# First-layer experts in order of their counts, with narrower column blocks, and a buffer fill moved into the recurrence

## The chip, the cores and the metric

The program runs on one core of one Trainium2 chip. The metric is the device time of one execution in microseconds. The kernel before took 592.91 us (median of 3 runs, 591.63 to 594.31).

## The reference

Three stages follow one another. A linear recurrence with state (4 batches, 8 heads, 768 steps, head size 48) gives 3072 tokens of 384 values. A first mixture of experts skips about half of the tokens and sends each of the others to one of 8 experts. A second mixture sends every token to one of 8 experts and keeps only the gated expert output.

```python
state = w[None, :, :, None] * state + np.einsum('bhd,bhe->bhde', kt, vt)   # per step
do_compute = x @ w_skip > 0                    # first mixture only
e_idx = np.argmax(xc @ w_gate, axis=1)
h = np.maximum(xc[mask] @ w1[e], 0.0)          # 384 -> 1024
y[mask] = gate_w[mask, None] * (h @ w2[e])     # 1024 -> 384
out[do_compute] = xc + y                       # second mixture: out[mask] = gate * y
```

With the inputs drawn here, 1490 tokens are not skipped. The first mixture's experts get 190, 182, 205, 159, 189, 184, 188 and 193 of them. Of expert 0's tokens, 126 lie in the first 2048 and 64 behind. The tokens of the second mixture's expert 0 are 188 skipped ones and 175 others.

## The kernel before, in words

The tokens of an expert are gathered through memory. `route` works out a slot for each token, and indirect DMAs from the POOL queue (`scatter`, line 271) write the rows into the buffers `xs1` (first mixture, 256 slots for each expert) and `xs2` (second mixture). The slots that get no token must hold the empty row `zrow`, so both buffers are first filled with it (`prefill`, line 256, on the SP queue). `xs1` is filled in iterations 3 to 8 of the recurrence, in 16 blocks of 128 rows. `xs2` has 29 such blocks; 13 are filled in `first_expert` and 16 in job 1.

The recurrence (`attention`) runs 24 iterations of 128 tokens. Each one loads its r, k and v on the SP queue (lines 439 and 443), several iterations ahead.

The experts run as a list of `jobs`. Expert 0 of the first mixture is done by `first_expert` in plain float32, 160 slots early and 96 late. Jobs 1 to 7 are the other seven experts with 256 slots each, jobs 8 and 9 the two halves of the second mixture's expert 0 (256 slots each), job 10 its expert 1 with 448 slots, and jobs 11 to 16 its experts 2 to 7 in the order of their counts (`by_count`), with 448 to 384 slots.

A job splits each operand into a high and a low float32r part. `gemm1` (line 1059) does 8 groups of 9 products (3 blocks of the contraction, 3 pairs of parts), with a block of 128x128 weights as the stationary operand and the job's slots as the moving columns, so 72 products whose width is the number of slots. `gemm2` (line 1082) does 24 products for each tile of up to 128 slots, with the slots as the stationary operand and 384 moving columns: 48 for two tiles. After each small group `work` is called. It converts one piece of the next expert's weights (`conv_w`, lines 877 and 878), starts the load of the one after (`load_w`, lines 858 and 860), runs steps of `route`, loads the rows of the next job (`load_rows`, line 1022, at step k = 2) and transposes them (`trans`, line 1034, from k = 9 on).

The order on each engine and queue is the order of the program text. The SP queue therefore handles weights, rows and fills strictly in turn, and an entry that waits holds back all behind it. If a count is over its slots, a flag sends the run to the slow path `general`.

Of the kernel before, what the change touches and what calls it, by code (L numbers as in the profile page):

```python
# [24 lines left out]
E = 8  # L25
# [31 lines left out]
PRE2A = 13  # L57
PF2 = range(1, 16, 2)
# [124 lines left out]
def attn_moe_moe_kernel(ctx: ExitStack, tc: tile.TileContext, t, out):  # L183
# [29 lines left out]
    eid = const.tile([1, NR], I32, name="eid")  # L213
    wg = const.tile([128, KB, WGC], F32, name="wg")
# [14 lines left out]
    def setup_consts2():  # L229
        P.iota(rev, pattern=[[-1, 8]], base=8, channel_multiplier=0, allow_small_or_imprecise_dtypes=True)  # L230
        P.memset(ecap, NOSLOT)
        for v in range(3):
            P.iota(ecap[0:1, v, 0:8], pattern=[[CAP1, 8]], base=0, channel_multiplier=0, allow_small_or_imprecise_dtypes=True)
            P.iota(ecap[0:1, v, 8:16], pattern=[[CAP2, 8]], base=2 * CAPS - CAP2, channel_multiplier=0, allow_small_or_imprecise_dtypes=True)
            P.memset(ecap[0:1, v, 8:9], float(CAPS if v == 2 else 0))
        P.memset(ecap[0:1, 1, 0:1], float(CAPA))
        P.memset(cum, 0.0)
        P.memset(caps[:, 1:8], float(CAP1))
        P.memset(caps[:, 9:16], float(CAP2))
        P.memset(caps[:, 0:1], float(CAPL))  # L240
        P.memset(caps[:, 17:18], float(CAPA))
        P.memset(caps[:, 8:9], float(CAPS))
        P.memset(caps[:, 18:19], float(CAPS))
# [3 lines left out]
        for i, c in enumerate(CAPR):  # L247
            P.memset(caps_r[:, i:i + 1], float(c))
# [155 lines left out]
    def attention():  # L404
        with ExitStack() as actx:
# [321 lines left out]
            for n in range(NT):  # L727
# [105 lines left out]
    def expert(n):  # L833

        if n not in regs:
            r = n - 2 * E + NR
            regs[n] = nc.values_load(eid[0:1, r:r + 1], engines=[mybir.EngineType.SP], min_val=E - NR, max_val=E - 1)
        return regs[n]

    def load_w(n, j):  # L840
# [4 lines left out]
        if n >= 2 * E - NR:  # L845
            e = expert(n)
# [35 lines left out]
    def post1(rows, i, m, p):  # L882
        V.scalar_tensor_tensor(
            out=rows[:, i, 0:DM], in0=p, scalar=rows[:, i, G1:G1 + 1], in1=rows[:, i, 0:DM], op0=ALU.mult, op1=ALU.add)
# [12 lines left out]
    def post2(rows, cap, k, i, m, p):  # L897
        o = rows[0:m, i, 0:DM]
        g = rows[0:m, i, G2:G2 + 1]
        if k == 0:  # L900
            nf, half = divmod(cap, 128)
# [4 lines left out]
        if m < 128:  # L906
# [4 lines left out]
        else:  # L911
            A.activation(out=o, in_=p, func=ACTF.Copy, scale=g)  # L912
# [7 lines left out]
    def first_rows(a, b):  # L920
        for i in range(2):
            lo, hi = max(a, i * 128), min(b, i * 128 + 128)
            if lo < hi:
                nc.sync.dma_start(out=rows0[lo - i * 128:hi - i * 128, i], in_=xs1[lo:hi])
# [18 lines left out]
    def first_2(i, q):  # L943
        if q == 0:
            acc[0] = psf.tile([128, 512], F32, tag="g2", bufs=2, name="g2")[:, 0:DM]
        for fb in (2 * q, 2 * q + 1):
            T.matmul(acc[0], lhsT=h0[:, fb, i * 128:i * 128 + 128], rhs=stage[0, 3 + fb // 3][:, fb % 3], start=fb == 0, stop=fb == FB - 1)
        if q == 3:
            post1(rows0, i, 128, acc[0])
# [3 lines left out]
    def first_expert():  # L953
# [30 lines left out]
        first_T(ps_g.tile([128, 512], F32, tag="tp", name="f_ps"), (0, 1, 2), CAPA, CAP1)  # L984
        for fb in range(FB):
            first_1(fb, CAPA, CAP1)
# [12 lines left out]
    jobs = [(0, n, n * CAP1, CAP1) for n in range(E)] + [(1, E, 0, CAPS), (1, E, CAPS, CAPS)]  # L999
# [5 lines left out]
    def tiles_of(cap):  # L1005

        nf, half = divmod(cap, 128)
# [5 lines left out]
    def load_rows(j):  # L1013
        l, n, base, cap = jobs[j]
        nf, half = divmod(cap, 128)
        small = j <= LAST_S
        x = pools["rows" if small else "rows2"].tile([128, nf + (half > 0), ROW], F32, tag="rows", bufs=3 if small else 2, name="rows")
        eng = nc.sync
        if base is None:
            base = expert(n) * CAP2 + (2 * CAPS - CAP2)  # L1020
# [6 lines left out]
    def trans(j, kb):  # L1027
        l, n, base, cap = jobs[j]
        if kb == 0:
            ps = (first, pools["rows"]) if j <= LAST_S else (pools["rows2"],) * 2  # L1030
            xT[j] = tuple(p.tile([128, KB, cap], F32R, tag=t, bufs=1, name=t) for p, t in zip(ps, ("xh", "xl")))
        tp = ps_g.tile([128, 512], F32, tag="lt" if kb == 1 else "tp", name="xt_ps")
        for i, m in tiles_of(cap):
# [6 lines left out]
    def gemm1(j, fb):  # L1040
# [5 lines left out]
        full = cap - cap % 128  # L1046
        if fb == 0:
# [7 lines left out]
            hT[j] = [p.tile([128, FB, full], F32R, tag=t, bufs=1, name=t) for p, t in zip(ps, ("hh", "hl"))] + extra  # L1055
# [10 lines left out]
    def gemm2(j, k, i, m, q):  # L1066
# [8 lines left out]
        for fb in (2 * q, 2 * q + 1):  # L1075
            if m < 128:
# [4 lines left out]
            for x, (a, b) in enumerate(((hh, w2h), (hh, w2l), (hl, w2h))):  # L1081
                T.matmul(p, lhsT=a[:, fb, r], rhs=b[:, fb], start=(fb == 0 and x == 0), stop=(fb == FB - 1 and x == 2))  # L1082
        if q == 3:
            if l:
                post2(rows[j], cap, k, i, m, p)
# [33 lines left out]
    def work(j, k):  # L1119
# [4 lines left out]
        big = len(tiles_of(cap))  # L1124
# [32 lines left out]
    def job(j):  # L1157
# [4 lines left out]
        for k, (i, m) in enumerate(tiles_of(cap)):  # L1162
# [4 lines left out]
    def by_count(tot):  # L1167

        over = ids_p.tile([1, 19], F32, tag="over", name="over")
        key, rank, place, c = (ids_p.tile([1, 1, NR], F32, tag=n, name=n)[:, 0] for n in ("key", "rank", "place", "cnt"))  # L1170
        m, s = (ids_p.tile([1, NR, NR], F32, tag=n, name=n) for n in ("m", "s"))
        last = slice(2 * E - NR, 2 * E)
# [5 lines left out]
        V.tensor_tensor(out=over, in0=tot, in1=caps, op=ALU.is_gt)  # L1178
        yield "dve"
        V.tensor_copy(out=c, in_=tot[:, last])  # L1180
        yield "dve"
        V.scalar_tensor_tensor(out=key, in0=c, scalar=8.0, in1=key_i, op0=ALU.mult, op1=ALU.add)
# [11 lines left out]
        V.tensor_copy(out=eid, in_=place)  # L1194
        yield "dve"
        V.tensor_tensor(out=s, in0=m, in1=rows_(c), op=ALU.mult)
# [3 lines left out]
        V.tensor_tensor(out=place, in0=place, in1=caps_r, op=ALU.is_gt)  # L1200
        yield "dve"
        V.tensor_tensor(out=over[:, last], in0=over[:, last], in1=place, op=ALU.max)
# [3 lines left out]
    with tc.manual_schedule():  # L1206
# [15 lines left out]
        start(by_count(tot))  # L1222
# [47 lines left out]
```

## Time and profile before

| what | value |
|---|---|
| median of 3 runs | 592.91 us (591.63 to 594.31) |
| the profiled execution: its time, its span | 599.21 us, 597.5 us |
| TensorE busy, mean granted clock | 564.1 us (94%), 0.962 |
| VectorE, ScalarE, GpSimd busy | 361.0, 269.2, 207.1 us |
| recurrence (up to the first product of the first expert) | up to 167.7 us |
| first expert | 167.7 to 194.4 us |
| jobs 1 to 9 | 194.4 to 379.4 us |
| jobs 10 to 16 | 379.4 to 586.5 us |

All times within the run are counted from the start of the span. TensorE's busy share counts a product until its modelled end, so products overlap; the pace of the engine is read from the distance of two starts. The tables of stretches give for each the busy time of every engine, the granted clock of TensorE (1.00 is 2.4 GHz, 0.50 is 1.2 GHz) and the share of the 16 DMA engines in use.

### The profile page before, as it was taken

What the parts mean: (1) busy time and instruction counts of PE and PEld (TensorE: products, weight loads), DVE (VectorE), ACT (ScalarE), POOL (GpSimd) and SP (SyncE); (2) the same over time, 40 slices, a digit from 0 to 9 for tenths busy, and PEclk for the clock granted to TensorE, in tenths of its full rate; (3) what the DMA queues carried; (4) which work ended last, traced back from release to release, by engine and by line L of the source; (5) the groups of instructions that cost most, each with busy time, mean ns of one, the idle gap of its engine ahead of it and who ended that gap; (6) DMA issues with size and microseconds to landing.
All of it is one profiled execution on the core that took longest, in us unless ns stands there. A gap on an engine that the chain in (4) does not pass through costs nothing. (4 is left out here: it accounts for less than half of the span.)

```text
span 597.5 us, 14565 instructions
## 1 busy us (share of the span) xinstructions
PE 564.1 (94%) x5947; PEld 508.0 (85%) x5947; DVE 361.0 (60%) x749; ACT 269.2 (45%) x536; POOL 207.1 (35%) x215
## 2 busy tenths in 40 slices
PE   7999889999989889999999999999999999999992
PEld 4788778788777789999899899998989898999992
DVE  7999999999344638666766635443334345455210
ACT  6344444443244535545564425544534454545320
POOL 6532144351332113688742412223231404142301
PEclk8889999889789989999999999999999999999997
DMA  7858755590535996577766631676466574742100
GB/s 157 206 151 265 227 160 144 165 303 15 181 120 161 356 378 199 203 240 234 240 204 214 199 112 71 195 245 209 154 186 214 150 255 143 255 140 78 38 15 27
DMA packets 57484, 107.66 MB, mean 180 GB/s; under 512 B 7052, under 2 KB 40840, under 8 KB 57408
## 3 DMA queue, kind: packets, MB, share of 16 engines
q1 hardware_dynamic: 51504, 94.82, 51.3%
q0 software_dynamic: 5904, 11.82, 5.3%
q8 instruction: 49, 0.80, 0.6%
q14 instruction: 27, 0.22, 0.1%
HBM read 85.86 MB, written 26.96 MB: 189 GB/s over the span
## 5 line engine op out<-in xcount | busy, mean ns | idle before, releaser
L1059 PE MATMUL g<-xh,w1h 128*128 128x256 f32 (+3 forms) x384 | 122.8, 320 | 0.0
L1059 PE MATMUL g<-xh,w1l 128*128 128x256 f32 (+3 forms) x384 | 120.0, 312 | 0.0
L1059 PE MATMUL g<-xl,w1h 128*128 128x256 f32 (+3 forms) x384 | 119.5, 311 | 0.1
L1061 DVE SCALAR_TENSOR_TENSOR hl<-g,hh 128x256 fp32r<-128x256 f32 (+1 forms) x128 | 61.3, 482 | 89.7 <-ACT hh L1060 87.0
L1082 PE MATMUL g<-w2h,hh 128*128 128x384 f32 x312 | 110.0, 353 | 0.0
L1082 PE MATMUL g<-w2h,hl 128*128 128x384 f32 x312 | 106.1, 340 | 0.0
L1082 PE MATMUL g<-w2l,hh 128*128 128x384 f32 x312 | 105.8, 339 | 0.0
L1060 ACT ACTIVATE hh<-g 128x256 fp32r<-128x256 f32 (+1 forms) x128 | 55.2, 432 | 65.9 <-PE g L1059 61.6
L1059 PEld LDWEIGHTS g<-xh,w1h 128*128 128x128 f32 x384 | 72.1, 188 | 4.5 <-DVE hl L1061 1.6
L878 POOL TENSOR_TENSOR w1l<-s,w1h 128x1024 fp32r<-128x1024 f32 x14 | 33.5, 2394 | 119.8 <-issue 108.7
L1059 PEld LDWEIGHTS g<-xl,w1h 128*128 128x128 f32 x384 | 72.3, 188 | 1.5 <-DVE xl L1038 0.3
L1059 PEld LDWEIGHTS g<-xh,w1l 128*128 128x128 f32 x384 | 72.2, 188 | 1.3
L271 POOL DMA_INDIRECT xs<-xall,idx_all x48 | 54.1, 1128 | 43.0 <-DVE cum L349 30.0
L1082 PEld LDWEIGHTS g<-w2h,hh 128*128 128x128 f32 x312 | 59.8, 192 | 3.1 <-issue 3.0
L1082 PEld LDWEIGHTS g<-w2l,hh 128*128 128x128 f32 x312 | 59.4, 191 | 0.1
L271 POOL DMA_INDIRECT out<-rows,ids x30 | 29.2, 974 | 87.0 <-ACT rows L912 62.3
L1082 PEld LDWEIGHTS g<-w2h,hl 128*128 128x128 f32 x312 | 59.0, 189 | 0.0
L1038 DVE TENSOR_TENSOR xl<-xt_ps,xh 128x256 fp32r<-128x256 f32 (+3 forms) x48 | 23.8, 496 | 55.5 <-ACT xh L1037 55.5
L539 POOL TENSOR_TENSOR RKP<-RK 112x512 f32<-112x512 f32 x22 | 30.4, 1382 | 71.4 <-DMA RK<-in_rk 47.4
L878 DVE TENSOR_TENSOR w1l<-s,w1h 128x1024 fp32r<-128x1024 f32 x28 | 34.3, 1226 | 20.9 <-ACT w1h L877 18.4
L878 DVE TENSOR_TENSOR w2l<-s,w2h 128x1152 fp32r<-128x1152 f32 x28 | 37.9, 1354 | 14.5 <-ACT w2h L877 14.0
L1037 ACT CAST xh<-xt_ps 128x256 fp32r<-128x256 f32 (+3 forms) x48 | 20.8, 433 | 54.7 <-PE xt_ps L1034 51.9
(196 smaller groups left out, 1081.5 us busy)
## 6 DMA issues: line engine op xcount, KB each, us to landing
s<-in_w1b SPq DMA_DIRECT2D x24, 512.0 KB
s<-in_w1a SPq DMA_DIRECT2D x21, 512.0 KB
RK<-in_rk SPq DMA_DIRECT2D x48, 192.0 KB
KV<-in_kv SPq DMA_DIRECT2D x24, 384.0 KB
s<-in_w2b SPq DMA_DIRECT2D x16, 576.0 KB
s<-in_w2a SPq DMA_DIRECT2D x14, 576.0 KB
w2r<-in_w2b SPq DMA_DIRECT2D x5, 1536.0 KB
xs<-zrow SPq DMA_DIRECT2D x7, 582.0 KB
```

Source lines behind the costliest of these rows:

```text
L271: i = P.indirect_dma_start(out=dst, out_offset=bass.IndirectOffsetOnAxis(ap=idx_col, axis=0), in_=src, in_offset=None, bounds_check=last, ...
L539: (V if n < 2 else P).tensor_tensor(out=RKP[x][0:112], in0=RK[i][:, 0], in1=RK[i][:, 1], op=ALU.mult)
L878: (P if j in POOL_LO else V).tensor_tensor(out=lo, in0=x, in1=hi.bitcast(F32), op=ALU.subtract)
L1037: A.copy(out=hi, in_=tp[:, 0:cap])
L1038: V.tensor_tensor(out=lo, in0=tp[:, 0:cap], in1=hi.bitcast(F32), op=ALU.subtract)
L1059: T.matmul(p, lhsT=a[:, kb, f], rhs=b[:, kb], start=(kb == 0 and i == 0), stop=(kb == KB - 1 and i == 2))
L1060: A.activation(out=hh[:, fb], in_=p[:, 0:full], func=ACTF.Relu)
L1061: V.scalar_tensor_tensor(out=hl[:, fb], in0=p[:, 0:full], scalar=0.0, in1=hh[:, fb].bitcast(F32), op0=ALU.max, op1=ALU.subtract)
L1082: T.matmul(p, lhsT=a[:, fb, r], rhs=b[:, fb], start=(fb == 0 and x == 0), stop=(fb == FB - 1 and x == 2))
```

## The change

It has four parts.

1. The number of computed slots in the first mixture becomes 240 for expert 1 and 256, 240, 224, 208, 208, 192 for experts 2 to 7, which are now taken in the order of their counts. The two halves of the second mixture's expert 0 get 240 each. The late part of expert 0 gets 80 in place of 96. The second tile of these jobs has 64 to 128 slots. Places in memory stay as they were.
2. For that order, a ranking of the six counts (`rank_1`) is put in `first_expert`, between the two parts of expert 0: one product and eleven small VectorE operations on one partition. SP reads the ranks into registers (`expert`), as it did for the second mixture.
3. All 29 blocks of `xs2` are filled one by one in iterations 8 to 22 of the recurrence, and no longer in `first_expert` and job 1.
4. The early rows of expert 0 are loaded from the POOL queue and no longer from SP.

```diff
-CAPA, CAPL = 160, 96
-CAPS = 256
+CAPA, CAPL = 160, 80
+CAPS, CAPT = 256, 240
+CAPR1 = (256, 240, 224, 208, 208, 192)
-PRE2A = 13
-PF2 = range(1, 16, 2)
+PF2 = range(8, 23)
...
-                first_rows(0, CAPA)
+                first_rows(0, CAPA, P)
...
                 if n in PF1:
                     q = PF1.index(n)
                     prefill(xs1, PRE1 * q // len(PF1), PRE1 * (q + 1) // len(PF1))
+                if n in PF2:
+                    q = PF2.index(n)
+                    for i in range(PRE2 * q // len(PF2), PRE2 * (q + 1) // len(PF2)):
+                        prefill(xs2, i, i + 1)
...
-            r = n - 2 * E + NR
-            regs[n] = nc.values_load(eid[0:1, r:r + 1], engines=[mybir.EngineType.SP], min_val=E - NR, max_val=E - 1)
+            ei, r = (eid1, n - E + NR) if n < E else (eid, n - 2 * E + NR)
+            regs[n] = nc.values_load(ei[0:1, r:r + 1], engines=[mybir.EngineType.SP], min_val=E - NR, max_val=E - 1)
...
         while not late[0]:
             drain()
             work(())
+        rank_1()
...
-            prefill(xs2, PRE2A * q // 4, PRE2A * (q + 1) // 4)
...
-    jobs = [(0, n, n * CAP1, CAP1) for n in range(E)] + [(1, E, 0, CAPS), (1, E, CAPS, CAPS)]
+    jobs = [(0, n, n * CAP1, CAPT) for n in range(E - NR)] + [(0, E - NR + r, None, c) for r, c in enumerate(CAPR1)]
+    jobs += [(1, E, 0, CAPT), (1, E, CAPS, CAPT)]
...
-            if j == 1 and k in PF2:
-                q, m = PF2.index(k), PRE2 - PRE2A
-                prefill(xs2, PRE2A + m * q // len(PF2), PRE2A + m * (q + 1) // len(PF2))
...
+    def rank_1():
+        tot = ps_g.tile([1, 19], F32, tag="lt", name="tot1")
+        T.matmul(tot, lhsT=ones[:, 0:1], rhs=cum, start=True, stop=True)
+        for _ in by_count(tot[:, E - NR:E], eid1, over1, caps_r1):
+            pass
```

## Rows read from the trace of the kernel before

**Rows 1.** Timeline of TensorE, products: start us, us, engine, line, operation, tiles, count.
```profile
204.31 0.34 PE L1082 MATMUL g<-w2h,hh 128*128 128x384 f32 x1
...
206.24 0.34 PE L1082 MATMUL g<-w2h,hl 128*128 128x384 f32 x1
211.01 0.48 PE L1034 MATMUL xt_ps<-ident,rows 128*128 128x128 f32 x2 [4.43 <-DMA rows<-xs]
...
220.23 0.36 PE L1059 MATMUL g<-xh,w1h 128*128 128x256 f32 x1
...
230.07 0.34 PE L1082 MATMUL g<-w2h,hh 128*128 128x384 f32 x1
...
239.83 0.36 PE L1059 MATMUL g<-xh,w1h 128*128 128x256 f32 x1
```

**Rows 2.** Table of stretches: PE, PEld, DVE, ACT, POOL busy, granted clock, DMA, GB/s.
```profile
195.00:201.50 6.50, 6.50 (x56) 5.90 (x56) 3.64 (x6) 4.53 (x10) 0.00 (x0) 1.00 1.06 345
211.00:214.80 3.80, 3.79 (x14) 3.76 (x14) 1.78 (x2) 1.43 (x2) 0.00 (x0) 0.55 1.05 382
```

**Rows 3.** Timeline of the SP queue, 188 to 201 us.
```profile
188.04 1.29 SPq L858 DMA_DIRECT2D s<-in_w1a  x3
189.38 2.25 SPq L256 DMA_DIRECT2D xs<-zrow  x4
...
199.84 1.04 SPq L256 DMA_DIRECT2D xs<-zrow  x1
200.93 0.46 SPq L1022 DMA_DIRECT2D rows<-xs  x1
```

**Rows 4.** Timeline of TensorE: first and last start of two runs of gemm1.
```profile
199.97 0.28 PE L1059 MATMUL g<-xl,w1h 128*128 128x256 f32 x1
...
201.86 0.28 PE L1059 MATMUL g<-xh,w1l 128*128 128x256 f32 x1
...
379.60 0.36 PE L1059 MATMUL g<-xl,w1h 128*128 128x448 f32 x1
...
387.90 0.37 PE L1059 MATMUL g<-xh,w1h 128*128 128x448 f32 x1
```

**Rows 5.** Timeline of TensorE: plain float32 products of the first expert.
```profile
172.82 2.63 PE L940 MATMUL g<-x,s 128*128 128x160 f32 x18
...
176.47 5.32 PE L947 MATMUL g<-s,h 128*128 128x384 f32 x16
```

**Rows 6.** Timeline of ScalarE: first and last of eight evictions, late part of expert 0.
```profile
183.80 0.25 ACT L941 ACTIVATE h<-g 128x96 f32<-128x96 f32 x1 [1.00 <-PE g L940]
...
188.49 0.25 ACT L941 ACTIVATE h<-g 128x96 f32<-128x96 f32 x1 [0.42 <-PE g L940]
```

**Rows 7.** Table of stretches in the recurrence, columns as in Rows 2.
```profile
58.50:65.00 6.50, 5.63 (x143) 4.78 (x140) 6.35 (x14) 1.77 (x5) 1.36 (x2) 1.00 0.85 263
...
91.00:97.50 6.50, 6.50 (x179) 5.80 (x177) 6.36 (x14) 2.92 (x7) 1.88 (x2) 1.00 0.45 117
```

**Rows 8.** Timelines of SP and ScalarE: last load of v, and its use.
```profile
126.03 0.57 SPq L443 DMA_DIRECT2D KV<-in_kv  x1
...
144.26 0.51 ACT L546 COPY VSO<-KV 64x384 f32<-64x384 f32 x1
```

**Rows 9.** Timelines of POOL, SP and TensorE: early rows of expert 0.
```profile
150.64 0.98 POOL L271 DMA_INDIRECT xs<-xall,idx_all  x1 [0.30 <-issue]
...
153.09 0.80 SPq L924 DMA_DIRECT2D rows<-xs  x2
...
162.74 1.37 PE L934 MATMUL f_ps<-ident,rows 128*128 128x128 f32 x6
```

**Rows 10.** Timeline of VectorE: its idle time in the first expert; one ranking operation.
```profile
190.49 0.43 DVE L1038 TENSOR_TENSOR xl<-xt_ps,xh 128x256 fp32r<-128x256 f32 x1 [4.96 <-ACT xh L1037]
...
364.14 0.18 DVE L1192 TENSOR_REDUCE place<-s 1x6 f32<-1x36 f32 x1
```

**Rows 11.** Instructions of one line: duration min/median/max ns, first and last start us.
```profile
L837 SPq TENSOR_LOAD <-eid x6: 269/278/478, 364.8 to 510.0; - x6
```

More of the change, by code (lines that the diff above doesn't have):

```diff
@@ L883, in post1 @@
         V.scalar_tensor_tensor(
-            out=rows[:, i, 0:DM], in0=p, scalar=rows[:, i, G1:G1 + 1], in1=rows[:, i, 0:DM], op0=ALU.mult, op1=ALU.add)
+            out=rows[0:m, i, 0:DM], in0=p[0:m], scalar=rows[0:m, i, G1:G1 + 1], in1=rows[0:m, i, 0:DM], op0=ALU.mult, op1=ALU.add)
         if i:
@@ L895, in attn_moe_moe_kernel, with post2 @@
     ids = {}
-    def post2(rows, cap, k, i, m, p):
+    def post2(rows, cap, k, i, m, p, small):
         o = rows[0:m, i, 0:DM]
@@ L905, in post2 @@
                 V.tensor_copy(out=ids[0][0:half, nf], in_=rows[0:half, nf, IDC:IDC + 1])
-        if m < 128:
+        if m < 128 and not small:
             A.copy(out=o, in_=p[m:2 * m])
@@ L1003, in attn_moe_moe_kernel, with row_tiles, tiles_of @@
     rows, xT, hT, pools, done = {}, {}, {}, {}, set()
-    def tiles_of(cap):
+    def row_tiles(cap, small):
+        return (2, 0) if small else divmod(cap, 128)
+    def tiles_of(j):
+        cap = jobs[j][3]
+        if j <= LAST_S:
+            return [(0, 128), (1, cap - 128)]
         nf, half = divmod(cap, 128)
@@ L1045, in gemm1 @@
         f = slice(fb * 128, fb * 128 + 128)
-        full = cap - cap % 128
+        full = cap if j <= LAST_S else cap - cap % 128
         if fb == 0:
@@ L1075, in gemm2 @@
         for fb in (2 * q, 2 * q + 1):
-            if m < 128:
+            if m < 128 and j > LAST_S:
                 ng = 128 // m
@@ L1081, in gemm2 @@
             for x, (a, b) in enumerate(((hh, w2h), (hh, w2l), (hl, w2h))):
-                T.matmul(p, lhsT=a[:, fb, r], rhs=b[:, fb], start=(fb == 0 and x == 0), stop=(fb == FB - 1 and x == 2))
+                T.matmul(p[0:m], lhsT=a[:, fb, r], rhs=b[:, fb], start=(fb == 0 and x == 0), stop=(fb == FB - 1 and x == 2))
         if q == 3:
             if l:
-                post2(rows[j], cap, k, i, m, p)
+                post2(rows[j], cap, k, i, m, p, j <= LAST_S)
             else:
@@ L1165, in job, with by_count @@
                 work(j, FB + 4 * k + q)
-    def by_count(tot):
-        over = ids_p.tile([1, 19], F32, tag="over", name="over")
-        key, rank, place, c = (ids_p.tile([1, 1, NR], F32, tag=n, name=n)[:, 0] for n in ("key", "rank", "place", "cnt"))
+    def by_count(c, ei, few, slots):
+        key, rank, place, cnt = (ids_p.tile([1, 1, NR], F32, tag=n, name=n)[:, 0] for n in ("key", "rank", "place", "cnt"))
         m, s = (ids_p.tile([1, NR, NR], F32, tag=n, name=n) for n in ("m", "s"))
-        last = slice(2 * E - NR, 2 * E)
         def rows_(x):
@@ L1177, in by_count @@
         yield "dve"
-        V.tensor_tensor(out=over, in0=tot, in1=caps, op=ALU.is_gt)
+        V.tensor_copy(out=cnt, in_=c)
         yield "dve"
-        V.tensor_copy(out=c, in_=tot[:, last])
-        yield "dve"
-        V.scalar_tensor_tensor(out=key, in0=c, scalar=8.0, in1=key_i, op0=ALU.mult, op1=ALU.add)
+        V.scalar_tensor_tensor(out=key, in0=cnt, scalar=8.0, in1=key_i, op0=ALU.mult, op1=ALU.add)
         yield "dve"
@@ L1193, in by_count @@
         yield "dve"
-        V.tensor_copy(out=eid, in_=place)
+        V.tensor_copy(out=ei, in_=place)
         yield "dve"
-        V.tensor_tensor(out=s, in0=m, in1=rows_(c), op=ALU.mult)
+        V.tensor_tensor(out=s, in0=m, in1=rows_(cnt), op=ALU.mult)
         yield "dve"
@@ L1199, in by_count, with rank_2 @@
         yield "dve"
-        V.tensor_tensor(out=place, in0=place, in1=caps_r, op=ALU.is_gt)
-        yield "dve"
-        V.tensor_tensor(out=over[:, last], in0=over[:, last], in1=place, op=ALU.max)
+        V.tensor_tensor(out=few, in0=place, in1=slots, op=ALU.is_gt)
+    def rank_1():
[3 more added lines that the diff above has]
+            pass
+    def rank_2(tot):
+        over = ids_p.tile([1, 19], F32, tag="over", name="over")
+        over2 = ids_p.tile([1, NR], F32, tag="over2", name="over2")
+        last = slice(2 * E - NR, 2 * E)
+        yield "dve"
+        V.tensor_tensor(out=over, in0=tot, in1=caps, op=ALU.is_gt)
+        yield from by_count(tot[:, last], eid, over2, caps_r)
+        for x in (over1, over2):
+            yield "dve"
+            V.tensor_tensor(out=over[:, last], in0=over[:, last], in1=x, op=ALU.max)
         yield "dve"
```

48 lines of the change are left out of this document (27 added, 21 removed).

## The prediction

> **What bounds the kernel now.** I read the table of busy times first, then the tables of stretches, then the timeline of the engine that is the bound in the stage that changes. In the recurrence VectorE is the bound: it is busy 6.35 of 6.50 us, in a stretch with much DMA traffic as in one with little [rows 7]. In the experts TensorE is: it is busy for the whole of a stretch in job 1, at the full 2.4 GHz [rows 2]. A change is therefore worth what it takes off TensorE's chain from 167.7 us on, and what it does to VectorE before.
>
> In that chain one hole stands out. The gemm2 phase of job 1 starts at 204.31 and job 2 starts at 220.23, so it takes 15.92 us. The same 48 products take 9.76 us in job 2 (230.07 to 239.83) [rows 1]. TensorE stops at 206.24 and starts again at 211.01 with the transposes for job 2. The wait is put down to the load of job 2's rows [rows 1]. Behind it the granted clock is 0.55, the 1.2 GHz level, up to 214.8 us [rows 2]. The hole and the slow products behind it together cost 15.92 - 9.76 = 6.2 us.
>
> Why the rows come late is seen on the SP queue. The load is issued at 200.93, so it takes some 10 us to arrive [rows 1, 3]. Ahead of it stand fills of the second buffer: four issues in the first expert (the 13 blocks) and one in job 1 (2 blocks) [rows 3], beside the weights. The DMA engines are at a share of 1.06 and move 345 GB/s [rows 2]. A block is 128 x 388 x 4 bytes = 0.199 MB; 15 of them are 3.0 MB, or 8.6 us at that rate.
>
> **Part 1: the fill moves.** Without the 8.6 us of fill ahead of it, the load takes 10.1 - 8.6 = 1.5 us, up to perhaps 3. It is wanted 206.4 - 200.9 = 5.5 us after its issue, so it is in time, with 2 us or more to spare. No hole then, and no fall of the clock: -6.2 us. If the wait only shrinks, the next ones in line are the weights for job 2, of which 3.1 MB share the same engines; alone they need 9 us of the 18 us between 188.04 and 206.24, so I do not expect them to show.
>
> What the 29 fills do in the recurrence: 2 blocks in an iteration of some 6 us are 67 GB/s. At 345 GB/s for a share of 1.06 that adds about 0.2 to a share of 0.45 [rows 2, 7]. The iterations with the first buffer's fill had 0.85 without VectorE falling idle [rows 7]. On SP each fill is one more issue of about 0.6 us (2.25 us for four) [rows 3], placed ahead of the loads of v. The last load of v is issued at 126.03 and its data first copied at 144.26, a lead of 18 us [rows 8]. I take 0. If that cover were gone, two issues in each of 15 iterations would be 15 x 1.1 = 17 us.
>
> **Part 2: the narrower products.** Two things can set the pace of gemm1: the moving columns, and the load of the 128x128 weights that each product needs. In rows 4 the distance of two starts is (201.86 - 199.97)/16 = 0.1181 us at 256 columns and (387.90 - 379.60)/41 = 0.2024 us at 448, so 0.44 ns for a column. That line gives 0.111, 0.104, 0.097 and 0.090 us at 240, 224, 208 and 192.
>
> The nearest row to a limit by the weights is the late part of expert 0: plain float32, 96 columns, the same 128x128 blocks of 4-byte weights. Its groups of six products follow one another at (188.49 - 183.80)/7 = 0.670 us, or 0.1117 us a product [rows 6]. The wider ones of that kind take 2.63/18 = 0.146 us at 160 columns and 5.32/16 = 0.333 us at 384 [rows 5], a line that gives 0.093 us at 96. The 0.1117 lies above it, so something other than columns sets it, and the weights are what is left. I take it as the floor for the float32r products too. It binds from 240 columns on.
>
> With the floor, each of the eight narrowed jobs (expert 1, five of the six ranked ones, the two halves; the ranked job with 256 stays) saves 72 x (0.1181 - 0.1117) = 0.46 us, together 3.7 us. Without it the 256 columns taken off in all save 256 x 72 x 0.44 ns = 8.1 us. The bounds of this part are 0 and 8.1; I take 3.7, by the row nearest in size of the weights.
>
> The Trainium skill (TensorE: Matmul & The Clock Gate, section LDWEIGHTS) puts the load of a stationary operand at its columns divided by 1.2, in ns, so 107 ns for 128 columns; it is a rule against narrowing below 256. The row of 0.1117 us agrees with it to 5 ns. With 0.1067 us for the floor this part would save 5.3 us as an estimate from that page, where the row gives 3.7.
>
> gemm2 saves nothing: its moving operand stays at 384 columns, and its pace, (206.24 - 204.31)/11 = 0.175 us over twelve products [rows 1], is above the floor whatever the number of slots. The late part of expert 0 goes from 96 to 80 columns and sits on the floor already: 0. Evictions and splits on ScalarE and VectorE become shorter, but beside TensorE.
>
> **Part 3: the ranking.** Eleven VectorE operations of about 0.18 us [rows 10], some 2.2 us with the gaps between dependent ones. VectorE is idle for 4.96 us up to 190.49 [rows 10], so from 185.5 on; the ranking ends there at about 187.7 and nothing behind it is held. The rank itself is the eighth operation, at 187.1, and SP's read into a register takes 0.27 to 0.48 us [rows 11]. SP needs it at 188.04 for the weights of the first ranked expert [rows 3], where today it waits for a buffer in any case. If it were late by 1 us, the four ranked loads behind it (weights and rows) would be too, against a cover of 2 us or more. The product that sums the counts is one of 19 columns, shorter than any in rows 4 (0.28 us); it stands before the transposes of the late rows. I take +0.3 us for it all.
>
> **Part 4: early rows on POOL.** Two issues at about 1 us [rows 9] in place of 0.80 on SP, at 153.1, when POOL has been through its scatters (the last at 150.64); the transposes that need them start at 162.74 [rows 9]. That leaves over 5 us. POOL waits meanwhile with nothing queued that is ready. SP is no longer held until 153.09, so the fills of the last iterations go out at once. 0.
>
> **Sum.** -6.2 - 3.7 + 0.3 = -9.6 us against the profiled execution of 599.21 us with its span of 597.5, so 589.6. That execution is 1.1% above the median of the runs; scaled, 9.6 becomes 9.5 and the time **583.4 us**.
>
> **Rivals.**
>
> *No floor.* If float32r weights load faster than the plain ones, part 2 gives 8.1: 592.9 - 6.2 - 8.1 + 0.3, scaled 579. Against it: rows 6. For it: the floor is read from another type. 0.15.
>
> *The hole is not there to be won.* The profiled execution is 6.3 us over the median, and the hole costs 6.2. If the timed runs have no hole, or if another load comes late in its place, part 2 alone is left: 592.9 - 3.4 = 589.5 us. Against it: the fill is 8.6 us of traffic in a stretch of full DMA engines, in any execution [rows 2]. 0.15.
>
> *Slower: float32r below 256 columns.* No float32r product in this trace has fewer than 256 moving columns. If below that point the chip worked through them as it does plain float32, a product would cost two passes: by the line of rows 5, 0.425 us at 240, 0.399, 0.372 and 0.345 at the others, in place of 0.118. That is 72 x (4 x 0.307 + 0.281 + 2 x 0.254 + 0.227) = 162 us, and the time 748 us. It decides at the first width under 256, so the ranked job with 256 would stay as it is and the other eight would all be slow. Against it: the pace is one line from 448 to 256 [rows 4] with no sign of a step. 0.10.
>
> *Slower: the recurrence pays.* The price above, 17 us, less the 9.6: 600 us. Against it: the stretch with 0.85 DMA share [rows 7] and the lead of 18 us [rows 8]. 0.05.
>
> *It does not do what it says* if a count exceeds its slots: then the slow path runs. With the drawn inputs the ranked counts are 205, 193, 189, 188, 184 and 159 for 256 to 192 slots, expert 1 has 182 and the halves 188 and 175 for 240, and 126 and 64 stand against 160 and 80. Under 0.01.
>
> **How the numbers follow.** The forecast itself has 0.54. It, the case of no floor and the one of no hole make 0.84 and lie between 579 and 589.5; with 1.5 us at either end the range is 577.5 to 591. About 0.5% (3 us) is what a measurement of this kernel can tell from no change, so faster means below 589.9. The case of no hole lies at that border and is shared: faster 0.77, same 0.08, slower 0.15.
>
> **What would show it.** Right: the gemm2 phase of job 1 at 9.8 us, the clock at 1.00 from 205 to 215 us, DMA share near 1 gone from 195 to 220 us; gemm1 at 0.112 us a product at every width from 240 to 192; the first job's start still at 194.4 us; VectorE without new waits for loads in the recurrence. Wrong: starts 0.3 to 0.4 us apart below 256 columns, a distance that falls to 0.09 us, a new wait for rows or weights in job 1, or a recurrence that ends later than before.

## The result: 584.45 us, and the profile after

The changed kernel takes 584.45 us (median of 4 runs, 582.82 to 586.06), beside 593.46 us for the kernel before in the same series (4 runs): 9.0 us less, a ratio of 0.985 [0.981, 0.989]. The forecast was 583.4 us. The profiled execution of after took 586.06 us with a span of 584.3 us; that of before 599.21 and 597.5.

| stretch of the profiled execution | before, us | after, us | difference |
|---|---|---|---|
| up to job 1 (its first product) | 194.39 | 192.82 | -1.6 |
| jobs 1 to 9 | 185.00 | 175.66 | -9.3 |
| of it: gemm1 phases, nine | 88.81 | 84.81 | -4.0 |
| of it: gemm2 phase of job 1 | 15.92 | 9.74 | -6.2 |
| of it: the other eight gemm2 phases | 80.27 | 81.11 | +0.8 |
| jobs 10 to 16, first to last product | 206.83 | 204.52 | -2.3 |
| TensorE busy; mean granted clock | 564.1; 0.962 | 551.1; 0.969 | |

A phase is counted from its first product to the first of the next phase, so it holds the transposes and waits that lie in it. From job 1 on the two profiled executions differ by 11.6 us (9.3 and 2.3), and the timed medians by 9.0. The gemm1 phase of job 3 is some 0.7 us long by a wait in before (10.52 us, where jobs 2, 4 and 5 have 9.83 or 9.84), and not in e12, a second execution of the same kernel (9.87).

The hole is closed. The timeline of TensorE of after (start us, us, engine, line, operation, tiles, count) around the gemm2 phase of job 1 answers [rows 1]:

```profile
202.37 0.34 PE L1100 MATMUL g<-w2h,hh 128*128 128x384 f32 x1
...
204.47 0.38 PE L1052 MATMUL xt_ps<-ident,rows 128*128 128x128 f32 x2
...
212.11 0.37 PE L1077 MATMUL g<-xh,w1h 128*128 128x256 f32 x1
```

The transposes of job 2's rows follow at 204.47 without a wait. The table of stretches of after (PE, PEld, DVE, ACT, POOL busy, granted clock, DMA share, GB/s) answers [rows 2]: 0.70 and 0.90 of the DMA engines where 1.06 and 1.05 stood, and the full clock where it was 0.55.

```profile
195.00:201.50 6.50, 6.50 (x59) 5.97 (x59) 4.23 (x7) 4.35 (x9) 0.00 (x0) 1.00 0.70 236
211.00:214.80 3.80, 3.80 (x32) 3.59 (x31) 1.69 (x4) 1.31 (x4) 2.17 (x3) 1.00 0.90 280
```

The pace of the narrow products, in TensorE's timeline at 192 columns, answers [rows 4]: (312.15 - 310.36)/16 = 0.112 us.

```profile
310.36 0.28 PE L1077 MATMUL g<-xl,w1h 128*128 128x192 f32 x1
...
312.15 0.27 PE L1077 MATMUL g<-xh,w1l 128*128 128x192 f32 x1
```

The ranking, in VectorE's timeline of after, answers [rows 10]: eleven operations from 184.00 to 186.11, and the next one behind them still waits for ScalarE.

```profile
184.00 0.15 DVE L1191 COPY cnt<-tot 1x6 f32<-1x6 f32 x1
...
185.96 0.15 DVE L1211 TENSOR_TENSOR over<-place,caps_r 1x6 f32<-1x6 f32 x1
188.92 0.41 DVE L1056 TENSOR_TENSOR xl<-xt_ps,xh 128x240 fp32r<-128x240 f32 x1 [2.81 <-ACT xh L1055]
```

One thing is new: TensorE waits for the early rows of expert 0. Timelines of TensorE, POOL and SP of after, which answer [rows 9] (brackets: idle before, and what ended it):

```profile
156.81 0.42 PE L271 MATMUL lt_ps<-xT,wg 128*32 128x128 f32 x6
161.53 0.30 PE L943 MATMUL f_ps<-ident,rows 128*128 128x128 f32 x1 [4.30 <-DMA rows<-xs]
162.84 1.61 PE L943 MATMUL f_ps<-ident,rows 32*128 32x32 f32 x5 [1.01 <-DMA rows<-xs]
...
150.21 0.98 POOL L276 DMA_INDIRECT xs<-xall,idx_all  x1 [0.30 <-issue]
156.93 1.14 POOL L933 DMA_DIRECT2D rows<-xs  x2 [5.74 <-DMA xs<-xall,idx_all]
...
149.20 1.29 SPq L867 DMA_DIRECT2D w1s<-in_w1a  x3
```

The last early scatter is issued at 150.21 as before at 150.64, but it lands only at 156.9. In before SP waited for the scatters and the three weight blocks of expert 1 came after the rows; now SP doesn't wait, and the 1.5 MB of weights start at 149.20 and fill the DMA engines while the scatters are under way. SP's timeline of before has them at 154.54, behind the rows at 153.09 [rows 9]:

```profile
154.54 1.29 SPq L858 DMA_DIRECT2D w1s<-in_w1a  x3
```

The stretch 150 to 155 us has a DMA share of 0.27 in the table of stretches of before

```profile
150.00:155.00 5.00, 4.65 (x48) 3.25 (x48) 0.57 (x2) 1.27 (x3) 1.31 (x2) 0.50 0.27 82
```

and of 0.94 in that of after:

```profile
150.00:155.00 5.00, 5.00 (x102) 4.19 (x104) 3.69 (x17) 2.24 (x6) 0.98 (x1) 1.00 0.94 329
```

### The profile page after: what moved, and what is told of

Same layout as the page of the kernel before. It is cut to its first block, busy times and chain, and to the rows that moved or that the text cites. A ratio compares the mean times of both kernels' runs of the same rounds, so it can differ in the third digit from the quotient of the medians.

```text
span 584.3 us, 14702 instructions
## 1 busy us (share of the span) xinstructions
PE 551.1 (94%) x5947; PEld 496.8 (85%) x5948; DVE 361.2 (62%) x761; ACT 266.1 (46%) x536; POOL 207.6 (36%) x224
## 5 line engine op out<-in xcount | busy, mean ns | idle before, releaser
L1077 PE MATMUL g<-xh,w1h 128*128 128x240 f32 (+7 forms) x384 | 121.3, 316 | 0.0
L1077 PE MATMUL g<-xl,w1h 128*128 128x240 f32 (+7 forms) x384 | 118.6, 309 | 0.1
L1077 PE MATMUL g<-xh,w1l 128*128 128x240 f32 (+7 forms) x384 | 118.5, 309 | 0.0
L1079 DVE SCALAR_TENSOR_TENSOR hl<-g,hh 128x384 fp32r<-128x384 f32 (+5 forms) x128 | 58.7, 464 | 85.2 <-ACT hh L1078 85.1
L1100 PE MATMUL g<-w2h,hh 128*128 128x384 f32 (+4 forms) x312 | 108.5, 348 | 0.0
L1100 PE MATMUL g<-w2h,hl 128*128 128x384 f32 (+4 forms) x312 | 105.0, 337 | 0.0
L1100 PE MATMUL g<-w2l,hh 128*128 128x384 f32 (+4 forms) x312 | 105.0, 336 | 0.0
L1100 PEld LDWEIGHTS g<-w2h,hh 128*128 128x128 f32 (+4 forms) x312 | 57.6, 185 | 4.0 <-issue 3.0
L1100 PEld LDWEIGHTS g<-w2l,hh 128*128 128x128 f32 (+4 forms) x312 | 57.1, 183 | 0.7
L1100 PEld LDWEIGHTS g<-w2h,hl 128*128 128x128 f32 (+4 forms) x312 | 56.9, 182 | 0.8
```

The costliest lines, as they stand in the source:

```text
L1077: T.matmul(p, lhsT=a[:, kb, f], rhs=b[:, kb], start=(kb == 0 and i == 0), stop=(kb == KB - 1 and i == 2))
L1079: V.scalar_tensor_tensor(out=hl[:, fb], in0=p[:, 0:full], scalar=0.0, in1=hh[:, fb].bitcast(F32), op0=ALU.max, op1=ALU.subtract)
L1100: T.matmul(p[0:m], lhsT=a[:, fb, r], rhs=b[:, fb], start=(fb == 0 and x == 0), stop=(fb == FB - 1 and x == 2))
```

## The experiments

The theory: the fill of the second buffer delays job 2's rows (6.2 us), the narrower products are held at 0.112 us by the load of 128 weight columns (3.7 us), and the rest is free. The rivals: no floor by the weights; a hole that belonged to one execution only; and, from the profile after, early rows on POOL that cost what the rest gains. All ratios are against the kernel before on the same chip. "After" names the changed kernel, from which the experiments start unless it is said otherwise.

| kernel | ratio to before, 95% | up to job 1, us | jobs 1 to 9, us | jobs 10 to 16, us |
|---|---|---|---|---|
| before | 1 | 194.4 | 185.0 | 206.8 |
| e12_before | 1.0015 [0.9974, 1.0056] | 186.8 | 185.8 | 207.1 |
| after | 0.9851 [0.9814, 0.9887] | 192.8 | 175.7 | 204.5 |
| e5_after | 0.9843 [0.9788, 0.9898] | 192.1 | 179.5 | 204.5 |
| e1_wide | 0.9941 [0.9903, 0.9979] | 193.9 | 180.0 | 204.5 |
| e3_all240 | 0.9891 [0.9854, 0.9928] | 191.0 | 176.8 | 204.5 |
| e2_oldfill | 1.0069 [1.0031, 1.0108] | 194.8 | 183.0 | 204.5 |
| e11_fillonly | 0.9974 [0.9932, 1.0017] | 201.5 | 179.0 | 207.1 |
| e4_sprows | 0.9839 [0.9792, 0.9887] | 191.2 | 176.5 | 204.5 |
| e6_pool_held | 0.9856 [0.9818, 0.9894] | 190.7 | 176.1 | 204.5 |
| e7_sprows_early | 0.9839 [0.9782, 0.9897] | 186.1 | 177.0 | 204.5 |
| e9_scatter3 | 0.9880 [0.9844, 0.9916] | 197.6 | 179.0 | 204.6 |
| e10_static | 0.9857 [0.9805, 0.9910] | 196.7 | 177.0 | 204.5 |

The last three columns are of each kernel's profiled execution. The start of job 1 is the least steady of them: 194.4 and 186.8 us in two executions of the same kernel before. In jobs 1 to 9, e5 takes 3.9 us more than after with the same code: its jobs 4 and 6 wait longer for rows (2.57 and 0.93 us against 0.94 and 0.27), and behind the first of these waits its granted clock is 0.60 (264.0 to 268.2 us). e9, e10 and e11 ran on a chip on which before itself takes 602.5 us.

**The widths: e1_wide and e3_all240.**

```diff
 # e1_wide
-CAPA, CAPL = 160, 80
-CAPS, CAPT = 256, 240
+CAPA, CAPL = 160, 96
+CAPS, CAPT = 256, 256
-CAPR1 = (256, 240, 224, 208, 208, 192)
+CAPR1 = (256, 256, 256, 256, 256, 256)
 # e3_all240
+CAPR1 = (256, 240, 240, 240, 240, 240)
```

> The changed kernel with all its first-layer jobs and both halves back at 256 computed slots and the late part of expert 0 at 96; the ranking, the moved fill and the early rows on POOL stay. If float32r products have a floor of about 0.112 us set by their 128x128 weights, the narrowing was worth 72 x 0.0064 us in each of eight jobs, so this takes 3 to 4 us more than the changed kernel: about 588. If columns alone set the pace, it was worth 8 us: about 592.5. gemm1 starts 0.118 us apart in the trace under both.

> The changed kernel with 240 slots in place of 224, 208, 208 and 192. With the floor: gemm1 at 0.112 to 0.113 us in these jobs as in the changed kernel, and the time within 0.5 us of it, 584 to 585. By columns: 128 columns x 72 x 0.44 ns = 4 us more, 588.5.

Measured: without the narrowing the gemm1 phases of jobs 1 to 9 sum to 88.89 us, with it to 84.81, so it is worth 4.1 us; by the ratios (0.9941 against 0.9851) 5.3 us, known to about 3. With 240 in place of 224, 208, 208 and 192 the sum is 85.31: the last 128 columns taken off bring 0.5 us, where the line without a floor has 72 x 128 x 0.44 ns = 4.1 us. The widths below 240 bring next to nothing in the trace. The ratio of e3 (0.9891 against 0.9851) is 2.4 us above that of after, which is inside what these runs leave open.

**The floor by itself: m1_pace.** A kernel that leaves out all the rest: runs of 40 products of one form, one after the other.

> Only rows of 40 products from resident operands, and a copy into the output; all of the model is left out. Distance of two starts at the full clock. If the load of 128 weight columns sets the floor: float32r with 128 weight columns near 0.112 us at 240 columns and every width below (down to 64), on the line of 0.44 ns a column above; with 64 weight columns the floor falls to about half, 0.055 to 0.06 us, so 192, 128 and 96 columns stay on the line. If the floor belongs to the product itself (a least time for a float32r product, whatever the weights), it stays at 0.112 with 64 weight columns. If narrow float32r products had a slow rate, the distance would rise below 256.

Groups of instructions of m1_pace by form (tile of weights, moving operand, count | busy us, mean ns of one):

```profile
L37 PE MATMUL p<-xr,wr 128*128 128x448 f32 x40 | 8.3, 365 | 0.0
L37 PE MATMUL p<-xr,wr 128*128 128x256 f32 x40 | 5.0, 283 | 0.0
L37 PE MATMUL p<-xr,wr 128*128 128x240 f32 x40 | 4.6, 275 | 0.0
L37 PE MATMUL p<-xr,wr 128*128 128x192 f32 x40 | 4.6, 274 | 0.0
L37 PE MATMUL p<-xr,wr 128*128 128x128 f32 x40 | 4.6, 275 | 0.0
...
L37 PE MATMUL p<-xr,wr 128*64 128x128 f32 x40 | 2.6, 222 | 0.0
L37 PE MATMUL p<-xr,wr 128*64 128x64 f32 x40 | 2.5, 223 | 0.0
...
L37 PE MATMUL p<-x,w 128*128 128x96 f32 x80 | 9.1, 275 | 0.0
L37 PE MATMUL p<-xb,wb 128*128 128x128 bf16 x40 | 2.4, 219 | 0.0
```

Forty products are 39 distances and one duration. With 128 weight columns float32r takes (4.6 - 0.275)/39 = 0.111 us at 240, 192 and 128 moving columns alike, and (5.0 - 0.283)/39 = 0.121 at 256. (Its 40 products at 64 moving columns take 4.8 us and so 0.116 each, with the granted clock at 0.94 in their stretch; all but three of their distances are 0.111 or 0.112 us.) With 64 weight columns the floor is (2.5 - 0.223)/39 = 0.058 us, about half, so it goes by the weights' columns. Plain float32 makes two passes (x80), each (9.1 - 0.275)/79 = 0.112 us: the floor of [rows 6] is the floor of float32r too, and below 256 columns no slower rate sets in. bf16 takes 0.056 us at 128 moving columns and is not held by it. The Trainium skill (TensorE: Matmul & The Clock Gate, section LDWEIGHTS) puts the load of weights at their columns divided by 1.2, in ns, which as an estimate is 107 ns for 128 columns and 53 ns for 64; the runs show 111 and 58 ns for 4-byte weights, some 5 ns above both.

**The fill: e2_oldfill, e11_fillonly, e12_before.** e2 puts the fill of after back to the first expert and job 1. e11 is the kernel before with the fill moved into iterations 6 to 20 and nothing else. e12 is the kernel before once more.

```diff
 # e2_oldfill (from after): the fill as in before
+PRE2A = 13
-PF2 = range(8, 23)
+PF2 = range(1, 16, 2)
...
 # e11_fillonly (from before)
-PRE2A = 13
-PF2 = range(1, 16, 2)
+PF2 = range(6, 21)
...
+                if n in PF2:
+                    q = PF2.index(n)
+                    for i in range(PRE2 * q // len(PF2), PRE2 * (q + 1) // len(PF2)):
+                        prefill(xs2, i, i + 1)
```

> The changed kernel with the 29 blocks of the second buffer filled where the kernel before filled them (13 in the first expert, 16 in job 1); everything else as changed. If the fill made the hole in job 1 in every execution, the trace shows a gemm2 phase of job 1 of 14 to 16 us, a wait for rows in it and the low clock behind it, and the time is 5 to 6 us above the changed kernel: about 590. If the hole was only in the profiled execution, the time stays near 584.5. If the fill in the recurrence cost something there, the time is less far above and the recurrence ends earlier than in the changed kernel.

> The kernel before with one part of the change alone, the fill of the second buffer in the recurrence (iterations 6 to 20, so that none stands behind the early rows, which stay on SP); widths as before, no ranking. If the fill made the hole in job 1: a gemm2 phase of job 1 of 9.8 us with the clock at 1.00, everything else as before, and 5 to 7 us under the kernel before, ratio 0.988 to 0.992. If the fill in the recurrence gives part of it back there: a ratio nearer 1, and VectorE waiting for loads in the recurrence.

> The kernel before, unchanged, profiled a second time and timed against itself. If the hole in the gemm2 phase of job 1 belongs to the kernel (forecast of part 1), this execution shows it again: the phase takes 14 to 16.5 us in place of 9.8, with a wait of over 3 us for the rows of job 2 and a granted clock under 0.8 behind it. If it belonged to the one execution profiled before (the rival that the hole is not there to be won), the phase takes 9.8 to 11 us, and the gain of moving the fill is then under 1 us in most runs. The ratio should be 1.000 within 0.004; how far it comes out from 1 shows what a comparison of this kind can tell. If low clock in the recurrence is what differs from run to run, its stretches of lower clock stand at other places than at 105 to 110, 130 to 135 and 150 to 155 us.

Measured: with the fill in its old place the gemm2 phase of job 1 takes 15.92 (before), 16.38 (e12) and 16.50 us (e2); in the ten kernels with the fill in the recurrence 9.69 to 9.77. The transposes of job 2's rows, in TensorE's timeline of e2,

```profile
211.91 0.66 PE L1050 MATMUL xt_ps<-ident,rows 128*128 128x128 f32 x2 [5.31 <-DMA rows<-xs]
```

in that of e12, the kernel before,

```profile
203.48 0.66 PE L1034 MATMUL xt_ps<-ident,rows 128*128 128x128 f32 x2 [4.47 <-DMA rows<-xs]
```

and, without a wait, in that of e11:

```profile
213.48 0.38 PE L1036 MATMUL xt_ps<-ident,rows 128*128 128x128 f32 x2
```

The table of stretches has, around that wait in e2,

```profile
210.00:215.00 5.00, 3.09 (x12) 3.12 (x13) 1.31 (x2) 1.42 (x2) 0.00 (x0) 0.66 1.05 390
```

and behind it in e12:

```profile
203.50:207.30 3.80, 3.80 (x13) 3.80 (x14) 1.78 (x2) 1.42 (x2) 0.00 (x0) 0.50 1.04 380
```

So the hole belongs to the kernel, with its fall to the 1.2 GHz level, and the fill makes it: moving the fill alone closes it. Nor is an execution with the hole an unusual one: that of e12 took 592.72 us, beside a median of 592.50. What closing it is worth in time the timed runs don't settle. Jobs 1 to 9 get 6.0 to 6.8 us shorter from before and e12 to e11, and 7.3 us from e2 to after (3.4 to e5, with its longer waits in jobs 4 and 6). Timed, the move gains 1.6 us on the kernel before (0.9974, up to 4.1 us by its interval), where 5 to 7 were expected; in after it is worth some 13 us (1.0069 against 0.9851 and 0.9843), where 5 to 6 were expected. Both expectations of the time failed. What makes the one smaller and the other larger than the hole must lie outside it, by the table most likely before job 1, where e11 starts job 1 4 to 5 us later than e9 and e10 on the same chip. The granted clock up to there goes the same way: 0.90 in e11 and 0.92 in e9 and e10, 0.90 in e2 and 0.92 in after. A cost of the fill in the recurrence would explain e11, but e10 has the same fill there and e9 the same 29 blocks two iterations later; the cause stays open.

**The early rows: e4_sprows, e6_pool_held, e7_sprows_early, e5_after.** e4 puts the load back on SP. e7 does too, and starts the fill two iterations earlier. e6 leaves the rows on POOL but puts one small load from `xs1` on SP, which must wait for the scatters and so holds the weights back. e5 is after once more, on the chip of e6 and e7.

```diff
 # e4_sprows, e7_sprows_early
-                first_rows(0, CAPA, P)
+                first_rows(0, CAPA)
 # e7_sprows_early also
-PF2 = range(8, 23)
+PF2 = range(6, 21)
 # e6_pool_held
                 first_rows(0, CAPA, P)
+                hold = ga_p.tile([1, 1], F32, name="hold")
+                nc.sync.dma_start(out=hold, in_=xs1[0:1, 0:1])
```

> The changed kernel with the early rows of expert 0 on the SP queue again, as in the kernel before. My forecast priced this part at 0. The trace of the changed kernel shows TensorE waiting 4.3 and 1.0 us for these rows, and SP issuing the weights of expert 1 (1.5 MB) at 149 us, ahead of the rows, where before they came after. If the POOL issue behind those weights is what makes the rows late, the rows on SP go out before the weights, the waits of 4.3 and 1.0 us go, and the time is 579 to 582. If they are late for the traffic of the moved fill, or the wait costs nothing in the end, the time stays at 584 to 585.

> The changed kernel itself again, beside the next two on one chip. Both theories: ratio to the kernel before near the 0.985 measured at first, 0.981 to 0.990. In the trace about 10 us between the last gate product of the recurrence and the first product of the first expert, against 5.3 us in the kernel before, with a wait for the early rows in between.

> The changed kernel, the early rows still on POOL, with one tiny load from the first buffer put on SP at the same place, so that SP waits for the early scatters as it did before the change and issues the weights of expert 1 behind them. If the 1.5 MB of weights ahead of the scatters and rows are the cause of the late rows, POOL's wait for the scatters falls from 5.7 to under 3 us, TensorE's wait for the rows shrinks to under 1 us, and the time is 3 to 5 us under the changed kernel's. If the issue on POOL is what is slow, the rows stay as late as in the changed kernel.

> The changed kernel with the early rows on SP and the fill two iterations earlier (6 to 20), so that no fill stands behind those rows. Weights ahead of the rows as the cause: no wait of TensorE for the early rows, 3 to 5 us under the changed kernel, ratio to the kernel before 0.976 to 0.981; it would beat both kernels. Rows priced at nothing, as in my forecast: the time of the changed kernel.

Measured: with the rows on SP the wait is gone. TensorE, SP and POOL of e4:

```profile
162.60 1.36 PE L943 MATMUL f_ps<-ident,rows 128*128 128x128 f32 x6
...
157.79 0.82 SPq L933 DMA_DIRECT2D rows<-xs  x2
...
161.98 1.41 SPq L867 DMA_DIRECT2D w1s<-in_w1a  x3
...
155.33 0.98 POOL L276 DMA_INDIRECT xs<-xall,idx_all  x1 [0.30 <-issue]
```

The last scatter is through 157.79 - 155.33 = 2.5 us after its issue (6.7 in after), since the weights stand behind the rows. From the last products of the gate ahead of these transposes (the start of their row in the timeline) to the first plain float32 product of the expert, e4 and e7 take 3.16 us, after 9.67, e1 6.19, e6 6.10, e5 4.95 (about 10 were expected), before 5.34. The 5.34 us of before hold no wait for rows; it waits 0.62 and 1.48 us there for ScalarE. The waits of TensorE for the early rows are therefore the better measure: with the rows on POOL 5.3 us in after, 5.2 in e2, 4.8 in e3, 1.8 in e1, 1.7 in e6, 1.2 in e5 and none in e9, and with the rows on SP none in any of the six kernels. In e6 POOL waits 2.07 us for the scatters (5.85 in e5), yet the rows are late all the same. POOL, SP and TensorE of e6:

```profile
152.60 1.14 POOL L935 DMA_DIRECT2D rows<-xs  x2 [2.07 <-DMA xs<-xall,idx_all]
...
154.95 2.59 SPq L869 DMA_DIRECT2D w1s<-in_w1a  x3
...
158.35 0.30 PE L945 MATMUL f_ps<-ident,rows 128*128 128x128 f32 x1 [0.23 <-DMA rows<-xs]
160.16 1.61 PE L945 MATMUL f_ps<-ident,rows 32*128 32x32 f32 x5 [1.51 <-DMA rows<-xs]
```

The order on SP therefore explains the wait for the scatters, and not the whole delay: in e6, with fills issued from 152.37 and weights from 154.95 us on, the first transposes start 158.35 - 152.60 = 5.8 us after the rows' issue, in e5 2.9 us after it. e9 has the rows on POOL and pays nothing. There SP comes to the weights only at 156.45, behind the rows; POOL waits 2.08 us for the scatters, and the transposes come only at 166.28. In time none of it is resolved: 0.9839, 0.9856 and 0.9839 against 0.9851 and 0.9843 for after, so the gains of some 3 to 5 us expected of e4, e6 and e7 did not show. The part costs up to 5.3 us of waiting in a trace and at most some 4 us in the timed runs.

**The waits in jobs 4 and 6: e9_scatter3, e10_static.** After waits 0.94 us in job 4 and 0.27 in job 6 for rows, e5 2.57 and 0.93. The theory was that the loads of those rows wait for a buffer, and that the scatter which frees it stands in POOL's queue behind the scatters of the skipped tokens, so e9 spaces the latter out. e10 does that too, and is a simpler kernel: rows on SP, an early fill, 240 slots in jobs 1 to 9 and no ranking of the first mixture.

```diff
 # e9_scatter3, e10_static
-            if skipped and j > 2 and k % 2 == 0:
+            if skipped and j > 2 and k % 3 == 0:
 # e10_static also
-    jobs = [(0, n, n * CAP1, CAPT) for n in range(E - NR)] + [(0, E - NR + r, None, c) for r, c in enumerate(CAPR1)]
+    jobs = [(0, n, n * CAP1, CAPT) for n in range(E)]
-                first_rows(0, CAPA, P)
+                first_rows(0, CAPA)
-PF2 = range(8, 23)
+PF2 = range(6, 21)
...
-        rank_1()
```

> The changed kernel with the scatters of the skipped tokens issued at every third step of jobs 3 to 6 in place of every second of jobs 3 to 5. In the traces of the changed kernel job 5's rows and job 7's come late (TensorE waits 0.9 to 2.6 us and 0.3 to 0.9 us) because their load waits for a row buffer whose scatter stands in POOL's queue behind those scatters, and POOL is nearly full in these jobs, which the narrower products have made shorter. If that is where part of the gain of the narrowing went, both waits go and the gemm2 phases of jobs 4 and 6 come to 9.7 us from 10.8, a gain of 1 to 3 us. If the loads are late for another reason (weights on the same engines), the waits stay.

> A candidate: the changed kernel with the early rows on SP, the fill in iterations 6 to 20, the scatters of the run before, and all seven experts of the first layer at 240 slots in their own order, so without the ranking. With the floor at 240 columns the widths under it are worth 0.5 us and the ranking costs about as much; the rows and the scatters give 1 to 5 us: ratio to the kernel before 0.972 to 0.982. If widths under 240 still gave 0.44 ns a column, it would be 4 us slower than with them: ratio 0.98 to 0.985.

Measured: the waits stay. TensorE of e9 in jobs 4 and 6, and POOL in job 4:

```profile
269.50 0.37 PE L1052 MATMUL xt_ps<-ident,rows 128*128 128x128 f32 x2 [1.22 <-DMA rows<-xs]
...
309.88 0.50 PE L1052 MATMUL xt_ps<-ident,rows 128*128 128x128 f32 x2 [1.02 <-DMA rows<-xs]
...
254.40 0.98 POOL L276 DMA_INDIRECT xs<-rows,idx  x1 [2.57 <-DVE cum L354]
```

POOL's queue does not hold those scatters: POOL is idle before the first of the two in job 4, 2.57 us in e9 and 0.53 in after, until VectorE is through with the slots of these rows. So the theory on the scatters of the skipped tokens falls. They cost something where they went: the gemm1 phases of jobs 4 to 6 take 30.3 us in e9 against 28.1 in after. Nor are the waits new: e12, the kernel before, waits 1.66 us in job 4. e10 is not told apart from after, and its expected ratio of 0.972 to 0.982 was not reached (0.9857). A fourth buffer for rows, which would test the rest of the theory, was not tried. No kernel here beats after by more than the measurement tells.

## Why the prediction was right, and where its working was not

**The total** was right: 9.0 us measured, 9.5 forecast. Its terms were not all right, and two that were left out have opposite signs. That it came within 0.5 us is in part luck: of the two large terms the timed runs give 1.6 and 5.3 us where 6.2 and 3.7 were forecast, each known to about 3.

**Part 1, the hole: -6.2 forecast.** The mechanism is shown: three executions with the fill in the old place have the hole, the fall of the clock and the late rows, ten without it have none. The size of the hole, 6.2 to 6.8 us, is that of the traces; the timed gain of the move by itself, 1.6 us (up to 4.1), is below it, and the effect in the other direction above it. The term stands as a reading of the trace and is not confirmed as a time. Inside it one size was off: without the fill ahead of it the load was to take 1.5 us, up to perhaps 3, and it landed 4.6 us after its issue in e5 and 4.8 in e1. So it is in time by 1.6 us (landed at 202.14, wanted at 203.70 in e5), not by 2 or more. The rival that the hole is not there to be won would have given 589.5 us; it loses by the three executions and by the total, while the timed gain of e11 alone would not have told the two apart.

**Part 2, the narrowing: -3.7 forecast.** The traces show 4.1 us against e1, the timed runs 5.3, known to about 3. Part of the 4.1 is that products of 256 columns are slower in e1 (0.120 us apart, as in job 2 of after) than in before (0.118); against the 88.08 us of e12 the nine phases get 3.3 us shorter. The step that carried it, a floor read from plain float32 in [rows 6] and used for float32r, is confirmed at every width: 0.111 to 0.113 us in after and 0.111 in m1_pace, against the 0.1117 taken. The rivals without a floor (579 us) and with a slow rate below 256 columns (748 us) fall with it.

**Part 3, the ranking: +0.3 forecast.** It ends at 186.11, and 2.81 us of idle time remain behind it. The rank is there at 185.61, SP begins to read it at 185.64, and its weights for the first ranked expert go out at 186.70, 6.12 us ahead of job 1, where before has 6.35 (188.04). The rank is thus just in time, where the forecast had it some 0.9 us early: it may hold these weights by some 0.2 us, and no wait of TensorE in job 1 follows from it. The +0.3 us were not measured by themselves.

**Part 4, the early rows: 0 forecast, and wrong.** The step that failed is "That leaves over 5 us", together with "SP is no longer held until 153.09, so the fills of the last iterations go out at once". It was true that SP is no longer held, but what goes out at once is also 1.5 MB of weights that stood behind the rows. They slow the scatters (6.7 us in place of 2.5) on which the rows wait. The margin itself was read from one execution whose recurrence ended late, with a clock of 0.50 at 150 to 155 us: from the issue of the rows to the transposes that need them before has 162.74 - 153.09 = 9.7 us, and e12, the same kernel, 158.81 - 154.31 = 4.5 us. TensorE stands for 5.3 us in after; against before the stretch is 9.67 - 5.34 = 4.3 us longer in this pair of traces, 0.9 with e1 and 0.4 shorter with e5, which has the same code as after. The cost in time is under what the runs resolve.

**What no step had: jobs 10 to 16, -2.3 us.** Their code is the same, but they take 204.5 us in all ten kernels built on after and 206.8 to 207.1 in the three built on before, on the same chip too (e9 and e10 against e11). The granted clock is 1.00 throughout in both. Most of the products are closer together. At 448 columns the distance is 0.2001 to 0.2003 us in all ten, and 0.2027 or 0.2066 in the three; in gemm2 it is mostly 0.173 against 0.175. The products of gemm1 at 384 columns differ by less than 0.0004 us, and those at 256 columns in jobs 1 to 9 go the other way. Over the same 41 distances in job 10 as in [rows 4] (8.30 us in before), TensorE's timeline has 8.20 us in after and 8.47 in e12:

```profile
368.69 0.36 PE L1077 MATMUL g<-xl,w1h 128*128 128x448 f32 x1
...
376.89 0.36 PE L1077 MATMUL g<-xh,w1h 128*128 128x448 f32 x1
```

```profile
372.87 0.37 PE L1059 MATMUL g<-xl,w1h 128*128 128x448 f32 x1
...
381.34 0.37 PE L1059 MATMUL g<-xh,w1h 128*128 128x448 f32 x1
```

It is not the fill (e2), the widths (e1), the ranking (e10) or the early rows (e4), since each of these kernels has it. What all ten keep of the change is, among other things, three more small constants ahead of the other tiles in memory; whether the tiles' places set the pace was not tried. They can't be the whole of it, since before and e12, which are one kernel, differ in this very job. A quarter of the gain thus comes from a source that was not foreseen and is not explained.

**The recurrence with its fills: 0 forecast.** Not refuted, not shown as a time. The sign that was named for it is absent: from 30 to 155 us VectorE waits for no load in any trace, with the fill there or without, while the DMA share of that stretch is 0.59 in before and 0.77 in after. The start of job 1 moves by 7.6 us between two executions of the same kernel, more than any cost of the fill that these runs could see. [rows 7], from which VectorE was read as the bound, are both stretches of full clock; at 130 to 135 us of before, where the clock is 0.50, TensorE is busy for all of the 5.00 us and VectorE for 4.08, so that reading doesn't hold there.

## What to carry to other kernels

Look for the floor of a product in the trace, in rows of another type or stage if need be, and stop narrowing where it binds: here at 240 columns, below which ranking and six widths bring 0.5 us. Before you price a transfer at nothing by its lead, read the lead in a second execution: here it was 9.7 us in one and 4.5 us in the other. When a load leaves a queue on which it waited, ask what stood behind it: that traffic starts earlier, and can slow the very transfer that the load waits for. Add up the phases of a whole execution before and after, the unchanged ones too: a total can be right with terms that cancel. And time a part by itself before you call it confirmed: a hole that the traces show can be worth another time than its length.

## What the runs showed of the hardware that was not expected

**The clock in the recurrence differs from execution to execution.** In before it is 0.66 at 105 to 110 us and 0.50 at 130 to 135; in e12, the same kernel, it is 1.00 at 105 to 110 and at 130 to 135, and 0.50 at 115 to 120; in after it is 0.50 at 30 to 35. TensorE is busy for the whole of each stretch of lower clock. The table of stretches has in before

```profile
105.00:110.00 5.00, 5.00 (x87) 4.03 (x86) 4.83 (x9) 2.45 (x5) 1.79 (x2) 0.66 0.69 181
130.00:135.00 5.00, 5.00 (x61) 3.90 (x61) 4.08 (x8) 2.45 (x5) 1.70 (x2) 0.50 0.94 341
```

in e12

```profile
105.00:110.00 5.00, 5.00 (x138) 4.41 (x138) 4.91 (x11) 1.54 (x4) 1.59 (x3) 1.00 0.69 196
115.00:120.00 5.00, 5.00 (x94) 4.88 (x92) 4.89 (x10) 0.37 (x1) 0.57 (x1) 0.50 0.34 101
```

and in after

```profile
30.00:35.00 5.00, 5.00 (x80) 4.49 (x78) 4.93 (x8) 2.44 (x5) 3.33 (x21) 0.50 0.60 157
```

Over 152 executions, each against the mean of its own kernel on its chip, time and mean granted clock go together with a correlation of -0.78, and 0.01 of clock with 3.7 us. The clock thus goes with about six tenths of the variance within one kernel, whose runs lie up to some 10 us apart, so that 6 to 12 runs leave an effect of 3 us unresolved. Which comes first, the slow clock or a late recurrence, is not shown.

**A float32r product has a floor by its weights' columns,** 0.111 us at 128 and 0.058 us at 64, while bf16 with 128 weight columns runs at 0.056 us.

**The same products can run 1 to 3% apart, in two kernels and in two executions of one,** at the same granted clock of 1.00 and without a difference in their form: at 448 columns 0.2001 us in job 10 of after, 0.2027 in before and 0.2066 in e12. The cause is open.
